# Two chunks split around a third, and attention output strips in turn, in a fused attention and MLP kernel

## The chip, the cores and the metric

The kernel runs on one core of a Trainium2 chip. Its engines are TensorE (PE, matrix products into PSUM), VectorE (DVE), ScalarE (ACT), GpSimd (POOL) and SyncE (SP, here the queue that issues every transfer). The metric is device time in microseconds (us) of one execution, as the median of several runs.

## The reference

A gated linear attention (4 batches, 8 heads, 768 time steps, head dimension 48) is followed by two MLPs over 3072 tokens of 384 features with 2048 hidden features: the first has the activation h * tanh(softplus(h)), the second relu(h) squared.

```python
for t in range(S):
    state = alpha[:, :, t, :, None] * state + np.einsum('bhd,bhe->bhde', k[:, :, t], v[:, :, t])
    y[:, :, t] = np.einsum('bhd,bhde->bhe', q[:, :, t], state)
...
h = x @ w_in
g = h * np.tanh(np.log1p(np.exp(h)))
x = g @ w_out
...
h = np.maximum(x @ w_in2, 0.0)
out = h * h @ w_out2
```

## The kernel before

**Staging.** Time is cut into 6 chunks (`c`) of 128 steps; a chunk holds 4 blocks, one per batch (`b`), so 512 tokens. The attention of one block is a handful of functions: `a_load` and `a_loadv` fetch alpha, k, q (one tile `akq`) and v; `a_prep`, `a_inv` and `a_k` run the cumulative products on DVE (two scans, three multiplications); `a_kT` transposes k on PE; `a_scores` forms the scores on PE and masks them on DVE (tiles `at`, two for a block); `a_y` forms the output on PE; `a_u` updates the running state `st`; `a_x` splits the output into a high and a low part (`xh`, `xl`), which the first MLP reads. Every f32 product of the MLPs is made from three matmuls of such parts.

**The MLP steps.** A step is one chunk `c` and one inner tile `f` of 128 hidden features (16 for each MLP). `h_mm` makes 9 matmuls into a PSUM bank `ph` (three banks), `mish1` to `mish3` or `relu1` run on ACT and DVE, `split_hi` and `split_lo` write `gh` and `gl`, and `out1` adds 9 matmuls into the accumulators `pc` of the chunk (`out2`, of the second MLP, 12 narrower ones). The first MLP has 96 steps in the order `STEPS1`, the second 96 in the order `STEPS`. The weights come as 64-bit floats in pairs of inner tiles and are turned into two f32 parts (`w_load`, `w_sign`, `w_abs`, `w_bits`, `w_split`, the last writing `whi` on ACT and `wlo` on DVE).

**What splits a chunk.** Before, chunk 0 runs its first 8 inner tiles, then chunk 1 all 16, then chunk 0 the other 8; its half sum waits in DRAM (`x2d`) and is fetched by `p_load`:

```python
STEPS1 = STEPS[:HALF] + STEPS[NF:2 * NF] + STEPS[HALF:NF] + STEPS[2 * NF:]
```

The tiles `xh` and `xl` have two buffers each, so that two chunks of attention output are held at a time.

**The order.** Nothing is issued as it is written. A `Plan` records every call, and its `order` gives each engine a fixed list: among the calls whose inputs it reckons ready, it picks by earliest start within `SLACK` and then by a key, from tables of numbers (`FIRST_AT`, `EARLY_AT`, `LATER_AT`, `WEIGHT_AT`, `MLP_AT`). The engines then run their lists in order, and SP its transfers.

**The attention output.** `a_y` fills a bank of 3 column blocks (`kk`) by 4 strips (`i`) of 32 output rows. In the first two blocks a strip takes a matmul from the state (not in chunk 0) and one from the masked scores of its head; in the third one from the state and two from scores. The strips are written one after the other:

```python
for i in range(4):
    ...
    if c > 0:
        nc.tensor.matmul(o, s2, qt[c, b][:, p, :], start=True, stop=False, skip_group_check=True)
    for h in heads:
        nc.tensor.matmul(o, w, at[c, b, j][:, p, :], ...)
```

Of the kernel before, what the change touches and what calls it, by code (L numbers as in the profile page):

```python
# [9 lines left out]
F32 = mybir.dt.float32  # L10
F32R = mybir.dt.float32r
# [16 lines left out]
LAG = 3  # L28
# [7 lines left out]
FIRST, EACH = -14.34, 4.47
FIRST_AT = dict(a_load=-8.92, a_loadv=-0.87, a_prep=-25.04, a_inv=-1.22, a_k=-40.25, a_kT=16.99, a_scores=-42.12, a_flag=-25.48, a_y=-7.03, a_u=-55.34, a_x=19.72)
EARLY_AT = dict(a_load=86.48, a_loadv=0.29, a_prep=-2.05, a_inv=1.20, a_k=-0.59, a_kT=-39.22, a_scores=-50.37, a_flag=29.17, a_y=-26.49, a_u=-16.63, a_x=-15.63)
LATER_AT = dict(a_load=-106.20, a_loadv=-63.70, a_prep=-101.21, a_inv=20.99, a_k=37.87, a_kT=-78.32, a_scores=-75.84, a_flag=23.67, a_y=2.78, a_u=-20.53, a_x=-24.76, b_load=-9.08, p_load=53.41)
WEIGHT_AT = dict(w_load=-16.99, w_sign=-7.37, w_abs=-52.56, w_bits=-0.61, w_split=-4.57)  # L40
MLP_AT = dict(mish1=42.39, mish2=0.64, mish3=1.90, hi=1.97, lo=-28.42, out=0.86)
EXP20 = 485165195.40979
NG = NF // 2

HALF = NF // 2
STEPS = [(c, f) for c in range(NBLK) for f in range(NF)]
STEPS1 = STEPS[:HALF] + STEPS[NF:2 * NF] + STEPS[HALF:NF] + STEPS[2 * NF:]
SEG = CH + 1
NALPHA = NP * SEG + 1
NROW = NALPHA + 2 * NP * CH  # L50
# [151 lines left out]
class Plan:  # L202
# [42 lines left out]
    def order(self):  # L245
        units = self.units
        users = {name: {i for i, _, _ in self.uses[name]} for name in self.tag_of}
        left = {name: len(x) for name, x in users.items()}
        nth, made, begun, freed = {}, {}, {}, {}
        for u in units:  # L250
            for name in u["new"]:
                tag = self.tag_of[name][0]
                nth[name] = made.get(tag, 0)
                made[tag] = nth[name] + 1
        held = [[] for _ in units]
        for name, x in users.items():
# [12 lines left out]

        def buffers(i):  # L270

            t, seen = 0.0, {}
            for name in units[i]["new"]:
                tag, bufs = self.tag_of[name]
                n = begun.get(tag, 0) + seen.get(tag, 0)
                seen[tag] = seen.get(tag, 0) + 1
                if nth[name] != n or len(freed.get(tag, [])) <= n - bufs:
                    return None
                if n >= bufs:
                    t = max(t, sorted(freed[tag])[n - bufs])  # L280
            return t

        for _ in units:
            picks = []
            for q, pool in ready.items():
                found = []
                for i in pool:
                    t = buffers(i)
                    if t is not None:
                        found.append((max(free[q], base[i], t, shared if units[i]["port"] else 0.0), units[i]["key"], i))  # L290
                if found:
                    first = min(found)[0]
                    pick = min((x for x in found if x[0] <= first + SLACK[q]), key=lambda x: x[1:])
                    picks.append((first, q, pick))
            _, q, (t, _, i) = min(picks, key=lambda x: x[0])
            u = units[i]
            ready[q].discard(i)
            start[i] = t
            free[q] = t + u["cost"] + (SWITCH if u["mode"] != mode and q == "P" else 0.0)
            mode = u["mode"] or mode  # L300
            done[i] = free[q] + u["late"]
            if u["port"]:
                shared = free[q] + (0.08 if q == "V" else 0.0)
            for name in u["new"]:
                tag = self.tag_of[name][0]
                begun[tag] = begun.get(tag, 0) + 1
            for name in held[i]:
                left[name] -= 1
                if not left[name]:
                    freed.setdefault(self.tag_of[name][0], []).append(max(done[j] for j in users[name]))  # L310
            for j in after[i]:
                base[j] = max(base[j], done[i] if i in units[j]["deps"] else start[i])
                wait[j] -= 1
                if not wait[j]:
                    ready[units[j]["queue"]].add(j)
        return sorted(range(len(units)), key=lambda i: start[i])
# [30 lines left out]
def price(queue, op, args, kw):  # L347
# [6 lines left out]
    if queue == "P":  # L354
        if op == "transpose":
            return 0.109, 0.2, False
        m, n = args[1].free_size(), args[2].free_size()
        if args[2].dtype == F32R:
            return n / 2200, 0.2, False
        return (0.085 if m == 32 else 0.052 if n == D else 0.107), 0.28, False  # L360
# [34 lines left out]
def fast_kernel(ctx, tc, flags, akq, v, w1i, w1o, w2i, w2o, out):  # L395
# [142 lines left out]
    def a_y(c, b):  # L538
        ps = abank(c, 2)
        for kk in range(NK):  # L540
            for i in range(4):
                o = ps[32 * i:32 * i + 32, CH * kk:CH * kk + CH]
                heads = (4 * kk + i,) if kk < 2 else (2 * i, 2 * i + 1)
                if c > 0:
                    p = heads[0] // 2
                    s2 = st[:, b, p, heads[0] % 2, CUT[heads[0] % 2][0]] if kk < 2 else st[:, b, p].rearrange("p j e -> p (j e)")[:, 32:64]
                    nc.tensor.matmul(o, s2, qt[c, b][:, p, :], start=True, stop=False, skip_group_check=True)
                for h in heads:
                    p, j = h // 2, h % 2
                    w = vt[c, b][:, h, CUT[j][1] if kk < 2 else CUT[j][2]]  # L550
                    nc.tensor.matmul(o, w, at[c, b, j][:, p, :], start=(c == 0 and h == heads[0]), stop=(h == heads[-1]), skip_group_check=True)
        yt[c, b] = ps

    def a_u(c, b):
# [25 lines left out]


    hps, ut, dy, gt, gh, gl = {}, {}, {}, {}, {}, {}
    acc, stage, part = {}, {}, None

    def mm3(ps, wpair, xhi, xlo, first, last):
        whi, wlo = wpair
# [42 lines left out]
        gl[c, f] = lo  # L629

    def out1(c, f):
        half = c == 0 and f >= HALF
        first, last = f in (0, HALF * half), f in (NF - 1, HALF - 1 if c == 0 else NF - 1)
        if first:
            acc[c] = [bank(psc, "pc") for _ in range(NK)]
        whi, wlo = wt[1, f]
# [2 lines left out]
            s = slice(128 * kk, 128 * kk + 128)  # L639
            mm3(acc[c][kk], (whi[:, s], wlo[:, s]), hi, lo, first, last)  # L640
        if last:
            t = part if half else stp.tile([128, NK, BT], F32, tag="stage", name="x2")
# [7 lines left out]
            nc.sync.dma_start(x2d[c], t)  # L650

    def p_load(c):
        nonlocal part
        part = stp.tile([128, NK, BT], F32, tag="stage", name="x2")
        nc.sync.dma_start(part, x2d[c])

    def b_load(c):
        hi = xp.tile([128, NK, BT], F32R, tag="xh", name="xh")
# [47 lines left out]
    with tc.manual_schedule():  # L706
# [13 lines left out]
        def at_step(t, fn, *args, key=None):  # L720
            name = fn.__name__
            if key is None:
                c, b = args[0], args[1] if len(args) > 1 else 0
                if c == 0 and name[0] == "a":
                    key = FIRST + EACH * b + FIRST_AT[name]
                else:
                    key = t + (EARLY_AT if 0 < c < 3 and name[0] == "a" else LATER_AT)[name]
            slots.setdefault(math.floor(t), []).append((fn, args, key))

        def wanted(m, g):  # L730
            return (STEPS if m > 1 else STEPS1).index((int(m < 2 and g >= NG // 2), 2 * g)) + LAG * (m % 2) + NA * (m // 2)

        def w_tasks(t, m, g):
            need = wanted(m, g)
# [15 lines left out]
            at_step(t + 5, a_x, 0, b)  # L750
        for c in range(1, NBLK):
            for b in range(B):
                t = (2 * b - 6, 2 * b + 17)[c - 1] if c < 3 else 16 * (c - 1) + 4 * b - 5
                at_step(max(t - 2, -7), a_load, c, b)
                at_step(max(t - 2, -7), a_loadv, c, b)
                at_step(t, a_prep, c, b)
# [111 lines left out]
```

## Time and profile before

| what | value |
|---|---|
| median of 3 runs | 965.78 us (963.88 to 966.77) |
| the profiled execution | 966.28 us, of which its span is 964.6 us |
| PE busy | 934.1 us |
| DVE busy | 637.3 us |
| ACT busy | 559.6 us |
| mean granted TensorE clock | 0.982 |

The span runs from the first to the last instruction of the profiled execution; 1.7 us of its own time lie outside it. PE is busy nearly throughout on the average, so that the time is to be read by stretches: where PE stands, and what it waits for there.

### The profile page before, as it was taken

What the parts mean: (1) busy time and instruction counts of PE and PEld (TensorE: products, weight loads), DVE (VectorE), ACT (ScalarE), POOL (GpSimd) and SP (SyncE); (2) the same over time, 40 slices, a digit from 0 to 9 for tenths busy, and PEclk for the clock granted to TensorE, in tenths of its full rate; (3) what the DMA queues carried; (4) which work ended last, traced back from release to release, by engine and by line L of the source; (5) the groups of instructions that cost most, each with busy time, mean ns of one, the idle gap of its engine ahead of it and who ended that gap; (6) DMA issues with size and microseconds to landing.
All of it is one profiled execution on the core that took longest, in us unless ns stands there. A gap on an engine that the chain in (4) does not pass through costs nothing.

```text
span 964.6 us, 14441 instructions
## 1 busy us (share of the span) xinstructions
PE 934.1 (97%) x5818; PEld 788.5 (82%) x5818; DVE 637.3 (66%) x1014; ACT 559.6 (58%) x1103; POOL 2.7 (0%) x10
## 2 busy tenths in 40 slices
PE   6888999999999999999999999999999999999996
PEld 5666777778888888878888889988999899999995
DVE  7899999998788887777679997343333343433332
ACT  4487998778666767677599865332332332422322
POOL 1000000000000000000000000000000000000000
PEclk7699999999999999999999999999999999999998
DMA  8145324340221211121032251010000100100001
GB/s 326 68 154 191 126 66 137 121 149 1 82 82 47 77 45 45 44 78 45 1 138 92 70 194 64 1 66 1 33 33 1 66 1 1 66 1 1 34 1 36
DMA packets 22075, 67.13 MB, mean 70 GB/s; under 512 B 1776, under 2 KB 4848, under 8 KB 22000
## 3 DMA queue, kind: packets, MB, share of 16 engines
q1 hardware_dynamic: 22000, 66.13, 19.6%
q8 instruction: 47, 0.77, 0.3%
q14 instruction: 28, 0.23, 0.1%
HBM read 55.90 MB, written 10.22 MB: 69 GB/s over the span
## 4 chain that ended last, share of the span: by engine, by line
PE 83%; ACT 7%; DVE 7%; issue 1%; DMA 1%; SPq 0%; DVEq 0%; ACTq 0%
PE ph L321 37%; PE pc L321 34%; PE pa L321 12%; ACT u L321 2%; ACT y L321 2%; ACT raw L321 1%; DVE akq L321 1%; ACT whi L321 1%; DVE raw L321 1%; DMA raw<-w1o 1%; DVE P L321 1%; DVE st L321 1%; ACT gh L321 1%; DVE gl L321 1%; ACT akq L321 1%
## 5 line engine op out<-in xcount | busy, mean ns | idle before, releaser
L321 PE MATMUL ph<-xh,wlo 128*128 128x512 f32 x576 | 230.1, 399 | 5.3 <-DVE g L321 2.7
L321 PE MATMUL ph<-xh,whi 128*128 128x512 f32 x576 | 228.0, 396 | 0.0
L321 PE MATMUL ph<-xl,whi 128*128 128x512 f32 x576 | 227.9, 396 | 0.0
L321 DVE TENSOR_TENSOR gl<-g,gh 128x512 fp32r<-128x512 f32 x192 | 131.9, 687 | 127.2 <-ACT gh L321 126.7
L321 ACT ACTIVATE u<-ph 128x512 f32<-128x512 f32 x192 | 113.8, 593 | 170.0 <-PE ph L321 163.4
L321 ACT ACTIVATE gh<-g 128x512 fp32r<-128x512 f32 x192 | 120.2, 627 | 135.1 <-PE pa L321 112.8
L321 DVE TENSOR_TENSOR g<-u,ph 128x512 f32<-128x512 f32 x96 | 66.0, 687 | 118.6 <-ACT u L321 118.6
L321 PEld LDWEIGHTS ph<-xh,wlo 128*128 128x128 f32 x576 | 108.7, 189 | 28.7 <-DVE g L321 4.4
L321 PEld LDWEIGHTS ph<-xh,whi 128*128 128x128 f32 x576 | 108.5, 188 | 25.4
L321 PEld LDWEIGHTS ph<-xl,whi 128*128 128x128 f32 x576 | 108.5, 188 | 20.6
L321 PE MATMUL pc<-gh,wlo 128*128 128x512 f32 x288 | 117.0, 406 | 0.9 <-ACT x L321 0.9
L321 PE MATMUL pc<-gh,whi 128*128 128x512 f32 x288 | 113.6, 394 | 0.0
L321 PE MATMUL pc<-gl,whi 128*128 128x512 f32 x288 | 113.1, 393 | 0.0
L321 DVE SCALAR_TENSOR_TENSOR u<-u,y 128x512 f32<-128x512 f32 x96 | 65.8, 686 | 50.4 <-ACT y L321 50.1
L321 PE MATMUL pc<-wlo,gh 128*128 128x384 f32 x288 | 97.0, 337 | 0.0
L321 PE MATMUL pc<-whi,gh 128*128 128x384 f32 x288 | 97.0, 337 | 0.0
L321 PE MATMUL pc<-whi,gl 128*128 128x384 f32 x288 | 96.9, 337 | 0.0
L321 DVE SCALAR_TENSOR_TENSOR g<-y,ph 128x512 f32<-128x512 f32 x96 | 65.4, 681 | 1.6
L321 PEld LDWEIGHTS pc<-gh,wlo 128*128 128x128 f32 x288 | 54.1, 188 | 14.8 <-ACT x L321 1.3
L321 DVE SCALAR_TENSOR_TENSOR y<-u,y 128x512 f32<-128x512 f32 x96 | 65.7, 685 | 0.7
L321 PEld LDWEIGHTS pc<-gh,whi 128*128 128x128 f32 x288 | 54.0, 187 | 13.2
L321 PEld LDWEIGHTS pc<-gl,whi 128*128 128x128 f32 x288 | 54.1, 188 | 12.1 <-DVE gl L321 0.6
(90 smaller groups left out, 1261.6 us busy)
## 6 DMA issues: line engine op xcount, KB each, us to landing
akq<-akq SPq DMA_DIRECT2D x20, 770.5 KB, 4.5
raw<-w1i SPq DMA_DIRECT2D x8, 768.0 KB, 4.6
v<-v SPq DMA_DIRECT2D x24, 256.0 KB, 4.4
raw<-w1o SPq DMA_DIRECT2D x8, 768.0 KB, 4.3
raw<-w2i SPq DMA_DIRECT2D x8, 768.0 KB, 4.4
raw<-w2o SPq DMA_DIRECT2D x8, 768.0 KB, 4.3
x2d<-x SPq DMA_DIRECT2D x7, 768.0 KB, 3.5
x<-x2d SPq DMA_DIRECT2D x7, 768.0 KB, 4.3
```

The lines of the kernel that those rows point to most:

```text
L321: method(*args, **kw)
```

## The change

Chunks 0 and 1 each run their first 8 inner tiles (steps 0 to 15), then chunk 2 all 16 (steps 16 to 31), then chunk 1 and chunk 0 their other 8 (steps 32 to 47); from chunk 3 on, the order stays. Since two buffers cannot hold three chunks, `x_keep` writes chunk 0's `xh` and `xl` to DRAM and `x_load` fetches them again, and chunk 1 now has a half sum to store and fetch as well. Chunk 2's attention is due 15 steps earlier than it was, the second half of the first MLP's weights 8 steps later. In `a_y` the four strips of a column block take turns: all state matmuls, then all first score matmuls, then all second ones. The planner's tables are new throughout, its price of a 32-row matmul is 0.06 in place of 0.085, and it counts two calls on PE, one behind the other, as free of the latency between them. The numbers of the tables decide the order and are not shown beyond a line.

```diff
-SLACK = dict(P=4.68, V=0.01, A=0.18, G=0.10, S=3.45)
+SLACK = dict(P=0.00, V=0.00, A=0.04, G=0.10, S=0.60)
...
-MLP_AT = dict(mish1=42.39, mish2=0.64, mish3=1.90, hi=1.97, lo=-28.42, out=0.86)
+MLP_AT = dict(mish1=-42.55, mish2=5.46, mish3=2.38, hi=8.43, lo=-0.03, out=3.78)
...
-HALF = NF // 2
+HALF, SPLIT = NF // 2, 2
 STEPS = [(c, f) for c in range(NBLK) for f in range(NF)]
-STEPS1 = STEPS[:HALF] + STEPS[NF:2 * NF] + STEPS[HALF:NF] + STEPS[2 * NF:]
+STEPS1 = [(c, f) for c in (0, 1) for f in range(HALF)] + [(2, f) for f in range(NF)]
+STEPS1 += [(c, f) for c in (1, 0) for f in range(HALF, NF)] + STEPS[3 * NF:]
...
+            groups = [(4 * kk + i,) if kk < 2 else (2 * i, 2 * i + 1) for i in range(4)]
+            o = [ps[32 * i:32 * i + 32, CH * kk:CH * kk + CH] for i in range(4)]
+            for i, heads in enumerate(groups if c > 0 else ()):
...
+                nc.tensor.matmul(o[i], s2, qt[c, b][:, p, :], start=True, stop=False, skip_group_check=True)
+            for n in range(len(groups[0])):
+                for i, heads in enumerate(groups):
...
-        half = c == 0 and f >= HALF
+        split = c < SPLIT
+        half = split and f >= HALF
...
+    def x_keep(c):
+        for x, d in zip((xh[c], xl[c]), x0d):
+            nc.sync.dma_start(d, x.bitcast(F32))
+
+    def x_load(c):
+        xh[c], xl[c] = (xp.tile([128, NK, BT], F32R, tag=name, name=name) for name in ("xh", "xl"))
+        for x, d in zip((xh[c], xl[c]), x0d):
+            nc.sync.dma_start(x.bitcast(F32), d)
...
-                t = (2 * b - 6, 2 * b + 17)[c - 1] if c < 3 else 16 * (c - 1) + 4 * b - 5
+                t = (2 * b - 6, 2 * b + 2, 2 * b + 33)[c - 1] if c < 4 else 16 * (c - 1) + 4 * b - 5
...
-        at_step(2 * NF - 2, p_load, 0)
+        at_step(HALF, x_keep, 0)
+        at_step(2 * NF, x_load, 0)
+        at_step(2 * NF + 4, p_load, 1)
+        at_step(2 * NF + HALF + 4, p_load, 0)
```

**On PE, in the third column block of `a_y`.** Before, for chunk 1's first block (`pa` is the output bank, `akq,st` the state matmul, `at,v` a score matmul), the first two of four strips:

```order
L321 MATMUL pa_209<-akq_159,st_109 32x128
L321 MATMUL pa_209<-at_197,v_160 32x128
L321 MATMUL pa_209<-at_198,v_160 32x128
L321 MATMUL pa_209<-akq_159,st_109 32x128
L321 MATMUL pa_209<-at_197,v_160 32x128
L321 MATMUL pa_209<-at_198,v_160 32x128
```

The same block in the change, with the last matmul of the second column block ahead of it and the state update behind it:

```order
L323 MATMUL pa_211<-at_200,v_162 32x128
L323 MATMUL pa_211<-akq_161,st_109 32x128 x4
L323 MATMUL pa_211<-at_199,v_162 32x128 x4
L323 MATMUL pa_211<-at_200,v_162 32x128 x4
L323 MATMUL pa_212<-v_162,kT_196 64x48 x8
```

Three matmuls of one strip stood together; now four of a kind, each of another strip, stand together.

**On DVE, ahead of the masked scores of a late attention block.** Before, the rows up to the second mask of chunk 2's last block (`at_488`, `at_489`), which stand behind 28 `h_mm` and 24 `out1` on PE; there are 293 rows up to here:

```order
L321 SCALAR_TENSOR_TENSOR y_454<-u_452,y_454 128x512
L321 TENSOR_SCALAR raw_995<-raw_995 128x768
L321 SCALAR_TENSOR_TENSOR g_469<-y_454,ph_451 128x512
L321 SCALAR_TENSOR_TENSOR raw_995<-raw_995 128x768
L321 SCALAR_TENSOR_TENSOR P_490<-akq_464,reset_108 128x516
L321 TENSOR_SCALAR x2_472<-pc_323 128x512
L321 TENSOR_TENSOR akq_464<-akq_464,P_490 128x512
L321 TENSOR_TENSOR at_488<-pa_486,mask_107 128x512
L321 TENSOR_TENSOR at_489<-pa_487,mask_107 128x512
```

In the change, the rows up to the second mask of chunk 3's first block (`at_571`, `at_572`), behind 33 `h_mm` and 27 `out1` on PE; there are 330 rows up to here:

```order
L323 TENSOR_TENSOR gl_504<-g_501,gh_503 128x512
L323 RECIPROCAL reset_108<-P_551 128x4
L323 SCALAR_TENSOR_TENSOR u_506<-u_506,y_508 128x512
L323 TENSOR_TENSOR gl_510<-g_507,gh_509 128x512
L323 SCALAR_TENSOR_TENSOR y_508<-u_506,y_508 128x512
L323 TENSOR_TENSOR akq_533<-akq_533,P_551 128x512
L323 TENSOR_TENSOR at_571<-pa_569,mask_107 128x512
L323 TENSOR_TENSOR at_572<-pa_570,mask_107 128x512
```

All of chunk 2's attention, which before stood between steps 18 and 28, now stands ahead of step 16, and chunk 3's last three blocks stand between steps 42 and 48.

**On SP, around the fetch of chunk 0's kept input.** In the change, with `x2_541` chunk 2's result and `x2_560` the half sum of chunk 1:

```order
L323 DMA raw_1018<-w2o 128x2x768
L323 DMA xh_524<-x0d0_110 128x1536
L323 DMA xl_525<-x0d1_111 128x1536
L323 DMA akq_552<-akq 128x1541
L323 DMA x2d2_114<-x2_541 128x1536
L323 DMA x2_560<-x2d1_113 128x1536
L323 DMA v_553<-v 128x512
```

The fetch waits for the last `h_mm` that reads chunk 2's `xh` (step 31), whose buffer it takes; the store of chunk 2's result, the fetch of chunk 1's half sum and chunk 3's later loads are queued behind it.

## Rows read from the trace of the kernel before

**Rows 1.** The page: span, then busy time, share and instructions of each engine.
```profile
span 964.6 us, 14441 instructions
...
PE 934.1 (97%) x5818; PEld 788.5 (82%) x5818; DVE 637.3 (66%) x1014; ACT 559.6 (58%) x1103; POOL 2.7 (0%) x10
```

**Rows 2.** Busy time by stretches: length, each engine (instructions), granted clock, DMA share.
```profile
0.00:42.49 42.49, 30.77 (x316) 24.53 (x317) 34.86 (x59) 19.31 (x40) 2.66 (x10) 0.73 0.57 206
42.49:133.71 91.22, 83.06 (x610) 64.72 (x609) 87.26 (x140) 76.53 (x152) 0.00 (x0) 0.98 0.43 150
133.71:201.13 67.42, 65.62 (x503) 51.53 (x503) 64.99 (x107) 56.56 (x117) 0.00 (x0) 1.00 0.32 109
201.13:225.14 24.01, 24.00 (x174) 19.24 (x174) 23.86 (x42) 17.19 (x37) 0.00 (x0) 1.00 0.29 102
225.14:547.40 322.26, 322.26 (x2174) 260.16 (x2173) 255.12 (x418) 235.99 (x475) 0.00 (x0) 1.00 0.17 61
```

**Rows 3.** PE's timeline at chunk 2's last block: start, duration, instruction, idle time and releaser.
```profile
201.13 0.42 PE L321 MATMUL pa<-akq,st 128*32 128x128 f32 x4 [0.77 <-DVE at L321]
```

**Rows 4.** PE's timeline through one attention output and the state update behind it.
```profile
239.85 0.45 PE L321 MATMUL pa<-akq,st 128*32 128x128 f32 x8
...
240.31 0.44 PE L321 MATMUL pa<-akq,st 128*32 128x128 f32 x8
...
240.75 0.38 PE L321 MATMUL pa<-akq,st 128*32 128x128 f32 x2
...
242.25 0.67 PE L321 MATMUL pa<-v,kT 128*64 128x48 f32 x16
242.85 0.50 PE L321 MATMUL pc<-gh,wlo 128*128 128x512 f32 x1
243.19 0.39 PE L321 MATMUL pc<-gl,whi 128*128 128x512 f32 x1
```

**Rows 5.** PE's timeline at a transposition of k and at the scores.
```profile
206.63 0.63 PE L321 MATMUL pa<-ident,akq 128*128 128x128 f32 x4
207.01 0.48 PE L321 MATMUL ph<-xh,wlo 128*128 128x512 f32 x1
...
209.30 1.16 PE L321 MATMUL pa<-akq 48*128 48x128 f32 x16
210.39 0.50 PE L321 MATMUL pc<-gh,wlo 128*128 128x512 f32 x1
```

**Rows 6.** PE's timeline at its last matmul of the second MLP.
```profile
955.30 0.34 PE L321 MATMUL pa<-whi,gh 128*128 128x384 f32 x1
```

**Rows 7.** The chain that ended last: one step's `h_mm`, one `out1`: start, us, what.
```profile
223.21 2.09 PE pc L321 x9
225.30 2.09 PE ph L321 x9
```

**Rows 8.** DVE's timeline where it runs without a break.
```profile
65.88 0.95 DVE L321 SCALAR_TENSOR_TENSOR raw<-raw 128x768 int32<-128x768 int32 x1
66.75 0.68 DVE L321 SCALAR_TENSOR_TENSOR y<-u,y 128x512 f32<-128x512 f32 x1
67.35 0.68 DVE L321 SCALAR_TENSOR_TENSOR u<-u,y 128x512 f32<-128x512 f32 x1
...
69.15 1.22 DVE L321 TENSOR_TENSOR_SCAN P<-akq,reset 128x516 f32<-128x516 f32 x1
70.29 0.66 DVE L321 SCALAR_TENSOR_TENSOR g<-y,ph 128x512 f32<-128x512 f32 x1
...
72.40 0.34 DVE L321 TENSOR_TENSOR st<-st,pa 64x192 f32<-64x192 f32 x1
72.67 0.68 DVE L321 TENSOR_TENSOR gl<-g,gh 128x512 fp32r<-128x512 f32 x1
```

**Rows 9.** DMA issues by kind: count, KB each, us from issue to landing.
```profile
x2d<-x SPq DMA_DIRECT2D x7, 768.0 KB, 3.5
x<-x2d SPq DMA_DIRECT2D x7, 768.0 KB, 4.3
```

More of the change, by code (lines that the diff above doesn't have):

```diff
@@ L32 @@
 BYTE_SHIFTS = range(8)
-SLACK = dict(P=4.68, V=0.01, A=0.18, G=0.10, S=3.45)
[L36 to L40, printed above, removed]
-MLP_AT = dict(mish1=42.39, mish2=0.64, mish3=1.90, hi=1.97, lo=-28.42, out=0.86)
+SLACK = dict(P=0.00, V=0.00, A=0.04, G=0.10, S=0.60)
+FIRST, EACH = -18.51, 1.95
+FIRST_AT = dict(a_load=-10.28, a_loadv=-6.32, a_prep=-5.60, a_inv=-5.08, a_k=-12.87, a_kT=22.41, a_scores=4.85, a_flag=79.31, a_y=-5.96, a_u=40.39, a_x=27.07)
+EARLY_AT = dict(a_load=-15.47, a_loadv=-42.21, a_prep=3.06, a_inv=3.92, a_k=-33.68, a_kT=-51.78, a_scores=-5.31, a_flag=-34.88, a_y=-38.93, a_u=3.94, a_x=-2.21)
+LATER_AT = dict(a_load=11.61, a_loadv=-15.13, a_prep=-5.26, a_inv=16.58, a_k=0.90, a_kT=-32.26, a_scores=-34.40, a_flag=-8.77, a_y=-1.60, a_u=-26.88, a_x=78.23, b_load=6.26, p_load=-50.04, x_keep=-25.45, x_load=-0.15)
+WEIGHT_AT = dict(w_load=-25.97, w_sign=-3.64, w_abs=53.00, w_bits=0.06, w_split=-0.32)
+MLP_AT = dict(mish1=-42.55, mish2=5.46, mish3=2.38, hi=8.43, lo=-0.03, out=3.78)
 EXP20 = 485165195.40979
 NG = NF // 2
-HALF = NF // 2
+HALF, SPLIT = NF // 2, 2
 STEPS = [(c, f) for c in range(NBLK) for f in range(NF)]
-STEPS1 = STEPS[:HALF] + STEPS[NF:2 * NF] + STEPS[HALF:NF] + STEPS[2 * NF:]
+STEPS1 = [(c, f) for c in (0, 1) for f in range(HALF)] + [(2, f) for f in range(NF)]
+STEPS1 += [(c, f) for c in (1, 0) for f in range(HALF, NF)] + STEPS[3 * NF:]
 SEG = CH + 1
@@ L311, in order @@
             for j in after[i]:
-                base[j] = max(base[j], done[i] if i in units[j]["deps"] else start[i])
+                same = units[j]["queue"] == "P" == u["queue"]
+                base[j] = max(base[j], free["P"] if same else done[i] if i in units[j]["deps"] else start[i])
                 wait[j] -= 1
@@ L359, in price @@
             return n / 2200, 0.2, False
-        return (0.085 if m == 32 else 0.052 if n == D else 0.107), 0.28, False
+        return (0.06 if m == 32 else 0.052 if n == D else 0.107), 0.28, False
     if queue == "S":
@@ L418, in fast_kernel @@
     st = const.tile([128, B, NP, 2, D], F32, name="st")
+    x0d = [dram.tile([128, NK, BT], F32, name=f"x0d{i}") for i in range(2)]
     x2d = [dram.tile([128, NK, BT], F32, name=f"x2d{i}") for i in range(NBLK)]
@@ L540, in a_y @@
         for kk in range(NK):
[L541 to L548, printed above, removed]
+            groups = [(4 * kk + i,) if kk < 2 else (2 * i, 2 * i + 1) for i in range(4)]
+            o = [ps[32 * i:32 * i + 32, CH * kk:CH * kk + CH] for i in range(4)]
+            for i, heads in enumerate(groups if c > 0 else ()):
+                p, j = heads[0] // 2, heads[0] % 2
+                s2 = st[:, b, p, j, CUT[j][0]] if kk < 2 else st[:, b, p].rearrange("p j e -> p (j e)")[:, 32:64]
+                nc.tensor.matmul(o[i], s2, qt[c, b][:, p, :], start=True, stop=False, skip_group_check=True)
+            for n in range(len(groups[0])):
+                for i, heads in enumerate(groups):
+                    h = heads[n]
                     p, j = h // 2, h % 2
                     w = vt[c, b][:, h, CUT[j][1] if kk < 2 else CUT[j][2]]
-                    nc.tensor.matmul(o, w, at[c, b, j][:, p, :], start=(c == 0 and h == heads[0]), stop=(h == heads[-1]), skip_group_check=True)
+                    nc.tensor.matmul(o[i], w, at[c, b, j][:, p, :], start=(c == 0 and n == 0), stop=(h == heads[-1]), skip_group_check=True)
         yt[c, b] = ps
@@ L582, in fast_kernel @@
     hps, ut, dy, gt, gh, gl = {}, {}, {}, {}, {}, {}
-    acc, stage, part = {}, {}, None
+    acc, stage, parts = {}, {}, {}
     def mm3(ps, wpair, xhi, xlo, first, last):
@@ L631, in out1 @@
     def out1(c, f):
-        half = c == 0 and f >= HALF
-        first, last = f in (0, HALF * half), f in (NF - 1, HALF - 1 if c == 0 else NF - 1)
+        split = c < SPLIT
+        half = split and f >= HALF
+        first, last = f == HALF * half, f in (NF - 1, HALF - 1 if split else NF - 1)
         if first:
@@ L641, in out1 @@
         if last:
-            t = part if half else stp.tile([128, NK, BT], F32, tag="stage", name="x2")
+            t = parts.pop(c) if half else stp.tile([128, NK, BT], F32, tag="stage", name="x2")
             for kk in range(NK):
@@ L652, in p_load @@
     def p_load(c):
-        nonlocal part
-        part = stp.tile([128, NK, BT], F32, tag="stage", name="x2")
-        nc.sync.dma_start(part, x2d[c])
+        parts[c] = stp.tile([128, NK, BT], F32, tag="stage", name="x2")
+        nc.sync.dma_start(parts[c], x2d[c])
+    def x_keep(c):
[5 more added lines that the diff above has]
+            nc.sync.dma_start(x.bitcast(F32), d)
     def b_load(c):
@@ L726, in at_step @@
                 else:
-                    key = t + (EARLY_AT if 0 < c < 3 and name[0] == "a" else LATER_AT)[name]
+                    key = t + (EARLY_AT if 0 < c < 4 and name[0] == "a" else LATER_AT)[name]
             slots.setdefault(math.floor(t), []).append((fn, args, key))
         def wanted(m, g):
-            return (STEPS if m > 1 else STEPS1).index((int(m < 2 and g >= NG // 2), 2 * g)) + LAG * (m % 2) + NA * (m // 2)
+            return (STEPS.index((0, 2 * g)) if m > 1 else min(n for n, (_, f) in enumerate(STEPS1) if f == 2 * g)) + LAG * (m % 2) + NA * (m // 2)
         def w_tasks(t, m, g):
```

## The prediction

> **What bounds the kernel now.** I read the page first: PE is busy for 97% of the span [rows 1]. Such an average hides where PE stands, so the stretches come next. The reader is to see that two kinds of time follow each other. Up to 201.13 us DVE is the engine without room: it is busy for 87.26 of 91.22 us and then for 64.99 of 67.42, while PE is busy for 83.06 and 65.62 [rows 2]. From 201.13 on PE is busy in 24.00 of 24.01 us and then in all of 322.26, with DVE at 255.12 [rows 2], and its last MLP matmul starts at 955.30 [rows 6]. The border is an event: at 201.13 chunk 2's last `a_y` begins after 0.77 us of waiting for the masked scores `at` of DVE [rows 3]. It is the last time that PE waits for DVE to any amount. So
>
> time = (when DVE lets PE past its last wait) + (PE work behind that) + tail.
>
> The last matmul starts at 955.30 and the next would start 0.17 later, so PE is done with the MLPs at 955.5; 9.1 us of span and 1.7 us outside it follow, and the change touches neither.
>
> **PE's prices.** One step's `h_mm` and one `out1` take 2.09 each [rows 7]; I use 2.09 for `out2` too. A transposition of k costs 207.01 - 206.63 = 0.38, the scores of a block 210.39 - 209.30 = 1.09 [rows 5], the state update 242.85 - 242.25 = 0.60, an `a_y` 242.25 - 239.85 = 2.40 [rows 4]. Where PE changes from narrow tiles to full ones, the next full matmul follows 0.34 later (243.19 - 242.85 [rows 4]) in place of 2.09/9 = 0.23, so each of these pieces costs 0.1 more.
>
> Check on before. At 201.13 the order has let 28 `h_mm` and 24 `out1` past; 164 and 168 are left, 332 x 2.09 = 693.9. Left of the attention: 13 `a_y` (31.2), 9 state updates (5.4), 12 transpositions (4.6), 12 scores (13.1), 46 edges (4.6), together 58.9. Sum 752.8; the trace has 955.5 - 201.1 = 754.4. So 1.6 us are lost in 750.
>
> **Term 1: strips in turn.** The 2.40 us of `a_y` are not spread evenly. The first two column blocks, 16 matmuls, take 240.75 - 239.85 = 0.90; the third, 12 matmuls, takes 242.25 - 240.75 = 1.50 [rows 4]. In the first two, eight records of state matmuls stand in one piece although the order alternates state and score: strips overtook one another there, with one matmul of a strip waiting behind another. With two waiting (the third block) they did not; the stretch of rows x1 and x2 there is a staggered queue. In turn, no strip ever has two matmuls in a row. I price the third block by the first two: 12 x 0.90/16 = 0.675. `a_y` becomes 1.575 and 0.825 us are saved, 20 times (chunk 0's `a_y` has no state matmul and keeps the pattern that already runs well): 16.5 us of PE work. Bounds: nothing, if the 1.50 has another reason, and no more than 16.5: a strip does its two matmuls of a block in 0.45, so its three take 0.675 even where all four strips run at once.
>
> The Trainium skill's page "TensorE: Matmul & The Clock Gate", section "Measured speedup vs the span model", gives three column tiles 2.38x, not 3x. If four strips overlapped only at that 79%, the third block would take 0.675/0.79 = 0.85 by an estimate from this page, and the saving would be 13 us. The rows of the first two blocks show no such loss, so I keep 16.5 and hold the other as a rival.
>
> **Term 2: when DVE lets PE past.** The change reorders DVE's work, so I count what stands ahead. Spacings of DVE instructions, start to start [rows 8]: 512 elements 0.60 (67.35 - 66.75), 768 elements 0.87 (66.75 - 65.88), a scan 1.14 (70.29 - 69.15), a state update 0.27 (72.67 - 72.40); 384 elements I estimate at 0.45 by their length.
>
> Before, up to the mask that PE waits for: 154 of 512 (92.4), 50 of 768 (43.5), 25 scans (28.5), 36 state updates (9.7), 11 of 384 (5.0), small ones 2.9; sum 182.0. DVE's busy time to 201.13 is 34.86 + 87.26 + 64.99 = 187.1 [rows 2], 2.8% more, and it idles for 7.6 us before 42.49 and 6.4 in the 158.6 us behind [rows 2].
>
> After, the comparable place is chunk 3's first `a_y`, behind 33 `h_mm` and 27 `out1`: DVE has 177 of 512 (106.2), 48 of 768 (41.8), 27 scans (30.8), 40 updates (10.8), 12 of 384 (5.4), small 2.2 ahead, sum 197.2. With the same 2.8%: 202.7; idle 7.6 at the start and 0.040 a us until then, 7.0. It is through at 217.3. Chunk 2's attention, now ahead of step 16, is four blocks more of DVE work there, but the second half of the weights moves behind it in exchange, and by step 32 the two sums have met again.
>
> PE work behind it: 159 + 165 = 324 x 2.09 = 677.2; 12 `a_y` at 1.575 (18.9), 8 state updates (4.8), 11 transpositions (4.2), 11 scores (12.0), 42 edges (4.2). Sum 721.3, with the 1.6 lost as before 722.9.
>
> **Term 3: chunk 3 squeezed.** From step 41 to 52 the order gives DVE 39.3 us of attention and 44 x 0.60 = 26.4 of activation, 65.7; PE has 66.7 us. Equal loads wait for each other now and then; I allow 1.0 us. Without DVE's lead there it would be 65.7 x 1.068 = 70.2 against 66.7 (2.8% and 0.040 as above), so at most 3.5.
>
> **Terms at nothing.** `x_keep`, `x_load` and the second half sum are six transfers of 768 KB at 3.5 or 4.3 us [rows 9]. They run beside transfers that take 0.43 to 0.29 of the engines' time [rows 2]. SP is in order, so what is queued behind matters. `x_keep` waits for chunk 0's last `xl`, which stands on DVE ahead of the masks of chunk 1's first block, while the next `akq` load behind it needs that block's buffer anyway. `x_load` can start after step 31, and step 40 needs it 36 us of PE work later; two transfers take 8.6. Without that cover PE would stand those 8.6 us at step 40. The half sums have as long.
>
> **Sum.** 217.3 + 722.9 + 1.0 = 941.2 against 955.5: 14.3 less, 952.0 for the profiled execution of 966.28. The median of the runs shown is 0.5 below that execution, so I predict **951.5**. A difference under 0.3% (2.9 us) is about what a measurement of this kernel can't tell from no change.
>
> **Rivals.**
> - *DVE waits less than before* in its new order: half the idle behind 42.49 gives 951.5 - 3.5 = 948. For: DVE's list has more attention to fill gaps with. Against: ACT, too, is busy 76.53 of 91.22 [rows 2], and DVE's gaps are waits for it.
> - *DVE bounds PE again* in steps 41 to 52: 951.5 + 2.5 = 954, with late loads behind the store of chunk 2's result up to 957. Chunk 3's last blocks come one right after the other, with scores masked only some 2 us ahead of `a_y`.
> - *The strips overlap in part*: 951.5 + 3.5 = 955.
> - *The strips gain nothing* and the change does not do what it says on PE: 951.5 + 16.5 = 968. Against it stand the 16 matmuls in 0.90 us.
> - *Slower*: chunk 2's attention and chunk 1's are both wanted in the first 16 steps, where DVE, ACT and PE hang on each other block by block. Each us that DVE idles more ahead of 217.3 is one us of the end. It decides at 14.3 more, 28.9 us of idle in place of 14.6; at 20 more the time is 971. For it speaks only that stretch's crowding; before, idle grew by 6.4 in 158.6 us.
>
> **How the numbers follow.** Chances: the forecast (948.5 to 954) 0.55; DVE again, or the strips in part (954 to 959), 0.20; DVE waits less (945 to 948.5) 0.12; idle growing by 8 to 14 us (959 to 965.8) 0.06; slower through DVE 0.04, strips without gain 0.03. The likeliest is 951.5. The range 946 to 959 leaves out 0.13 above and some 0.04 below; the likeliest case alone spans 948.5 to 954. Below 962.9 (faster by over 0.3%) lie 0.91, within 0.3% (to 968.7, strips without gain among them) 0.05, above 0.04.
>
> **What would show it.** An `a_y` of chunk 1 on should take 1.5 to 1.7 us on PE, its third block about 0.7. PE's last wait for `at` or `gl` of more than 0.5 us should lie at 212 to 222 us, and PE should be busy without a break behind it. `x_load` should land before 235. I am wrong in term 1 if `a_y` stays above 1.9; in term 2 if PE stands behind 225; in term 3 if it stands near steps 41 to 52 (about 250 to 330) for over 3 us.

## The result, and the profile after

The changed kernel takes 957.84 us (median of 4 runs, 955.87 to 958.36) against 965.25 of the kernel before (4 runs beside it): ratio 0.9919 [0.9897, 0.9941], 7.4 us faster. I had predicted 951.5, 14.3 less: the direction was right and half of the gain is missing; the time lies inside the range of 946 to 959, in the branch from 954 to 959 that had a chance of 0.20. The profiled execution took 958.34 us.

The page after, with the lines that answer to [rows 1]:

```profile
span 956.4 us, 14433 instructions
...
PE 927.8 (97%) x5818; PEld 780.4 (82%) x5818; DVE 636.3 (67%) x1017; ACT 554.2 (58%) x1103; POOL 2.7 (0%) x10
```

The stretches of [rows 2], now of the changed kernel (length, busy time of PE, its weight loads, DVE, ACT and POOL, granted clock, DMA share, GB/s):

```profile
0.00:42.49 42.49, 33.02 (x348) 26.98 (x352) 35.10 (x61) 18.36 (x40) 2.66 (x10) 0.64 0.66 242
42.49:133.71 91.22, 83.53 (x744) 64.81 (x736) 86.24 (x144) 70.80 (x146) 0.00 (x0) 0.91 0.42 148
133.71:201.13 67.42, 67.19 (x422) 53.32 (x421) 65.27 (x103) 59.28 (x121) 0.00 (x0) 1.00 0.34 114
201.13:225.14 24.01, 24.01 (x165) 19.16 (x165) 23.96 (x40) 21.39 (x46) 0.00 (x0) 1.00 0.47 165
225.14:547.40 322.26, 319.58 (x2142) 254.24 (x2141) 265.09 (x436) 237.72 (x482) 0.00 (x0) 1.00 0.21 72
```

Two things are new. In 42.49 to 133.71 the granted clock is 0.91 where it was 0.98. And behind 225.14, where PE was busy without a break before, it now stands for 322.26 - 319.58 = 2.7 us.

PE's timeline through one undisturbed `a_y`, to be read beside [rows 4] (a record group's start, duration, instruction), with the full matmul ahead of it:

```profile
323.08 0.40 PE L323 MATMUL pc<-gh,whi 128*128 128x512 f32 x1
323.41 0.43 PE L323 MATMUL pa<-akq,st 128*32 128x128 f32 x8
323.65 0.40 PE L323 MATMUL pa<-at,v 128*32 128x128 f32 x8
323.87 0.40 PE L323 MATMUL pa<-akq,st 128*32 128x128 f32 x8
324.09 0.40 PE L323 MATMUL pa<-at,v 128*32 128x128 f32 x8
324.31 0.40 PE L323 MATMUL pa<-akq,st 128*32 128x128 f32 x8
324.53 0.62 PE L323 MATMUL pa<-at,v 128*32 128x128 f32 x16
325.08 0.67 PE L323 MATMUL pa<-v,kT 128*64 128x48 f32 x16
```

It takes 325.08 - 323.41 = 1.67 us in place of 2.40. The third column block, 1.50 before, takes 325.08 - 324.31 = 0.77. Every group of four strips starts 0.22 to 0.24 behind the one ahead of it (two records a matmul), in the third block as in the first two. One full-width matmul of 128 columns takes as long in e8 below (24 in 5.28 us, 0.22 each), so the four strips overlap fully. The last row of the block takes 0.55: two groups at 0.22, and 0.11 on the way to the next piece.

PE's and DVE's timelines where chunk 3's first `a_y` begins (the place that answers to [rows 3]), and PE's last matmul ([rows 6]):

```profile
218.81 0.43 PE L323 MATMUL pa<-akq,st 128*32 128x128 f32 x8
...
947.35 0.34 PE L323 MATMUL pa<-whi,gh 128*128 128x384 f32 x1
```
```profile
216.90 1.28 DVE L323 TENSOR_TENSOR at<-pa,mask 128x512 f32<-128x512 f32 x2
```

The masks end at 216.90 + 1.28 = 218.18, PE comes at 218.81 and does not wait: there is no bracket with idle time at that row, where [rows 3] has 0.77.

**PE's lost time.** To see where time goes I take the start of a step's `h_mm` and subtract PE's work ahead of it at its durations in the traces (2.09 for `h_mm` and `out1`, 1.09, 0.38 and 0.60 for scores, transposition and state update, 1.67 or 2.40 for `a_y`, 1.23 for chunk 0's, 6.9 for the warm-up, 0.1 for each narrow piece). What is left is time that PE lost up to there, dummy matmuls of an experiment included. One profiled execution of each kernel (steps count from 0):

| kernel | step 8 | 16 | 42 | 58 | 180 | median us | ratio to before |
|---|---|---|---|---|---|---|---|
| before | 29.0 | 31.9 | 35.4 | 35.6 | 36.4 | 965.25 | |
| changed | 34.2 | 36.4 | 36.9 | 42.4 | 43.3 | 957.84 | 0.9919 |
| e1 | 31.5 | 34.5 | 40.7 | 41.5 | 42.9 | 958.75 | 0.9932 |
| e2 | 30.0 | 30.3 | 30.5 | 32.5 | 33.5 | 963.27 | 0.9986 |
| e3 | 31.8 | 34.6 | 35.5 | 38.2 | 39.2 | 954.05 | 0.9889 |
| e4 | 33.4 | 36.2 | 36.8 | 42.3 | 43.9 | 957.00 | 0.9909 |
| e5 | 29.4 | 32.5 | 33.0 | 36.0 | 36.9 | 954.04 | 0.9882 |
| e6 | 30.6 | 33.7 | 36.2 | 38.2 | 39.3 | 956.36 | 0.9906 |
| e7 | 31.2 | 34.3 | 35.2 | 37.6 | 38.6 | 955.37 | 0.9895 |
| e8 | 31.3 | 34.2 | 34.7 | 41.3 | 43.1 | 958.10 | 0.9925 |
| e9 | 31.9 | 34.8 | 35.7 | 39.4 | 40.4 | 956.94 | 0.9916 |
| e10 | 32.6 | 34.8 | 35.3 | 40.8 | 41.7 | 957.45 | 0.9918 |
| e11 | 30.6 | 33.7 | 34.2 | 39.7 | 40.7 | 954.93 | 0.9890 |
| e12 | 29.9 | 33.0 | 33.9 | 36.5 | 38.0 | 953.82 | 0.9878 |

The first two rows account for the result: twenty `a_y` save 20 x 0.73 = 14.6 us of PE work, and PE loses 43.3 - 36.4 = 6.9 us more, so 7.7 less; the profiled executions differ by 966.28 - 958.34 = 7.9. In the changed kernel PE loses nearly nothing between steps 16 and 42, and then 5.5 us between 42 and 58, where before lost 0.2.

The places in that stretch, by PE's timeline (idle time ahead of a row and what ended it in brackets):

```profile
287.95 0.63 PE L323 MATMUL pa<-ident,akq 128*128 128x128 f32 x4 [0.90 <-PE pa L323]
298.94 0.51 PE L323 MATMUL ph<-xl,whi 128*128 128x512 f32 x1 [0.40 <-DVE xl L323]
317.39 0.63 PE L323 MATMUL pa<-ident,akq 128*128 128x128 f32 x4 [0.56 <-PE pc L323]
347.63 0.63 PE L323 MATMUL pa<-ident,akq 128*128 128x128 f32 x4 [0.81 <-issue]
```

These four are 2.7 of the 5.5 us. Another 1.0 lies inside `a_y`, which there take up to 2.04 in place of 1.67 without a bracket. Of the remaining 1.8, some 0.8 is no waiting at all: the table prices a narrow piece at 0.1, but where it stands between full matmuls it costs about 0.1 at either end (323.08 to 323.41 above is 0.33, in place of 0.23). Between steps 42 and 58 the changed kernel's 27 narrow pieces stand in 20 separate groups; at the border prices of its undisturbed stretches that makes 3.5 us where the table counts 2.7. Before has 16 pieces in 12 groups there and spends 1.9 where the table counts 1.6. The last 1.0 is spread over full matmuls that start late, again without a bracket.

DVE's timeline ahead of the first of these places, and the scalings of k ahead of the third and the fourth:

```profile
283.77 0.68 DVE L323 SCALAR_TENSOR_TENSOR x<-pc,x 128x512 f32<-128x512 f32 x1
284.37 0.68 DVE L323 TENSOR_TENSOR gl<-g,gh 128x512 fp32r<-128x512 f32 x1
284.97 0.68 DVE L323 SCALAR_TENSOR_TENSOR x<-pc,x 128x512 f32<-128x512 f32 x1
285.57 1.22 DVE L323 TENSOR_TENSOR_SCAN akq<-akq,reset 128x516 f32<-128x516 f32 x1
286.71 0.53 DVE L323 TENSOR_TENSOR xl<-pa,xh 128x384 fp32r<-128x384 f32 x1
287.16 0.69 DVE L323 TENSOR_TENSOR akq<-akq 128x512 f32<-128x512 f32 x1
...
316.60 0.69 DVE L323 TENSOR_TENSOR akq<-akq 128x512 f32<-128x512 f32 x1
...
346.85 0.68 DVE L323 TENSOR_TENSOR akq<-akq 128x512 f32<-128x512 f32 x1
```

The transposition at 287.95 reads the k that DVE scales at 287.16 and finishes at 287.85; the profile names another instruction of PE, which had long been done. The other two transpositions, too, begin 0.10 behind the scaling of their k. DVE runs without a break ahead of each of the three, and ahead of the first two additions of chunk 1's half sum (`x<-pc,x`) stand in its queue.

### The profile page after: what moved, and what is told of

Same layout as the page of the kernel before. It is cut to its first block, busy times and chain, and to the rows that moved or that the text cites. A ratio compares the mean times of both kernels' runs of the same rounds, so it can differ in the third digit from the quotient of the medians.

```text
span 956.4 us, 14433 instructions
## 1 busy us (share of the span) xinstructions
PE 927.8 (97%) x5818; PEld 780.4 (82%) x5818; DVE 636.3 (67%) x1017; ACT 554.2 (58%) x1103; POOL 2.7 (0%) x10
## 4 chain that ended last, share of the span: by engine, by line
PE 82%; DVE 12%; ACT 2%; issue 1%; DMA 1%; SPq 0%
PE ph L323 39%; PE pc L323 34%; PE pa L323 10%; DVE akq L323 3%; DVE P L323 1%; DVE st L323 1%; DVE at L323 1%; DVE gl L323 1%; DVE y L323 1%; DVE g L323 1%; DVE u L323 1%; DVE raw L323 1%; DMA v<-v 1%; DMA raw<-w1i 1%; ACT u L323 1%
## 5 line engine op out<-in xcount | busy, mean ns | idle before, releaser
L323 PEld LDWEIGHTS ph<-xh,wlo 128*128 128x128 f32 x576 | 108.9, 189 | 29.9 <-DVE g L323 3.7
L323 DVE SCALAR_TENSOR_TENSOR u<-u,y 128x512 f32<-128x512 f32 x96 | 65.8, 686 | 34.4 <-ACT y L323 33.7
```

Source lines behind the costliest of these rows:

```text
L323: method(*args, **kw)
```

## Experiments: the two halves of the change apart

Only `a_y` is exchanged between the two kernels, by the lines of the diff above; every other instruction keeps its place in its own kernel's order.

**e1**, before with the new strips:

```diff
-            for i in range(4):
 ...
-                for h in heads:
 ...
+            for n in range(len(groups[0])):
+                for i, heads in enumerate(groups):
 ...
```

> The kernel before with its own order, tables and half sums, in which only the matmuls of a_y go to the four strips in turn; no other instruction moves. Theory A (strips give 0.73 us for each a_y, PE is the bound only behind 201 us there): the 13 a_y behind 201.13 us save 13 x 0.73 = 9.5 us, the 7 ahead of it hide behind DVE: 965.25 - 9.5 = 955.8, between 950.7 (all 20 count) and 957; that is as fast as the changed kernel or faster, so its new order gives nothing. Rival B (the new order is needed for the gain): 960 or more. Rival C (strips gain nothing): 965.

Measured 958.75 (0.9932 [0.9912, 0.9951]): 6.2 less than 964.99, the median of before in that comparison; the profiled executions differ by 966.28 - 958.01 = 8.3. The median lies between A's range (up to 957) and B's (960 or more). By the lost time A has the mechanism: up to step 42 it grows from 35.4 to 40.7, so the seven `a_y` there (7 x 0.73 = 5.1) gave nothing. A is too rich, as 1.2 us more are lost behind (2.2 in place of 1.0). C falls, and so does B: e1 is within 1 us of the changed kernel, with intervals that overlap, so most of the gain doesn't need the new order.

**e2**, the changed kernel with the old strips (the same edit backwards):

> The changed kernel with a_y's matmuls in their old order, strip by strip; no other instruction moves. Theory A: the 12 a_y behind 218.8 us cost 0.73 us more each, 8.8 us, less what hides in the 5.3 us that PE waits in steps 43 to 57 (up to four a_y, 2.9 us); those ahead of 152 us hide behind DVE: 957.84 + 5.9 to 8.8 = 963.7 to 966.6, so the new order alone is worth about nothing against 965.25. Rival B (the order carries the gain): under 961. Rival C: 957.8.

Measured 963.27 (0.9986 [0.9972, 0.9999]). The new order alone is worth 0.14%, and its interval only just excludes no gain; the strips on top of it are worth 963.27 - 957.84 = 5.4, just below what A gave: twelve `a_y` cost 8.8 us of PE work more, and 3.4 of it disappears in PE's waits, which between step 42 and the end are 3.0 in place of 6.4. The parts add: 0.9932 x 0.9986 = 0.9918.

The new order does something else than it seems. By step 42 it loses 5 us less than the old one (30.5 against 35.4, both with the old strips); behind step 42 it loses 3.0, the old one 1.0.

## Experiments: where steps 42 to 58 lose their time

**e3**, chunk 3's state updates early:

```diff
-                    at_step(t + 6, a_u, c, b)
+                    at_step(t + 6, a_u, c, b, key=t + 1 if c == 3 else None)
```

> The changed kernel in which chunk 3's four state updates have the key t + 1 in place of t + 9.94, so that the first one runs in step 34 in place of 43, and chunk 3's later blocks and chunk 4's first two come some 2 to 4 steps earlier, into the stretch in which DVE idles (steps 35 to 43, about 10 us). Theory A (the missing 6 us are PE's waits for a DVE that has too much to do in steps 43 to 57 because the attention comes late): 2 to 5 us less, 953 to 956. Rival D (the same work is just as crowded earlier): 957 to 959. Rival E (the missing time lies in the added transfers or in a_y): no change, 957.8.

Measured 954.05 (0.9889 [0.9869, 0.9909]): in A's range, and D and E fall. The loss between steps 42 and 58 is 2.7 in place of 5.5; this profile was also 1.8 us ahead at step 16, where both kernels are the same, so that not all of the 3.8 us comes from the key. The buffer `kT` is single (`ktp` has one), so what the next block's transposition gives can't be stored until this update has read it; with its key of 42.9 it held chunk 3's second block until step 43.

**e4**, the added transfers twice:

```diff
             nc.sync.dma_start(d, x.bitcast(F32))
+            nc.sync.dma_start(d, x.bitcast(F32))
 ...
             nc.sync.dma_start(x.bitcast(F32), d)
+            nc.sync.dma_start(x.bitcast(F32), d)
```

> The changed kernel in which each transfer of x_keep and of x_load is made twice (four more transfers of 768 KB on the same queue, 3.5 to 4.3 us each); PE's order is the same. Theory A (these transfers are hidden): 957.8, within 1.5. Rival E (they are what costs the missing 6 us, as loads queued behind them come late): 961 or more.

Measured 957.00 (0.9909 [0.9892, 0.9926]), inside A's range: the transfers are hidden, E falls again.

**e5**, five short scans:

```diff
+        if (3, 0) < (c, b) < (4, 2):
+            nc.units[-1]["calls"][0] = (..., (back[:, :8], back[:, :8], ...), ...)
```

The scan is priced in full by the planner, so that the order stays, and issued over 8 elements.

> The changed kernel in which five backward scans of DVE (chunk 3's blocks 1 to 3, chunk 4's blocks 0 and 1) run over 8 elements in place of 516: some 5 x 1.0 us less work for DVE between 264 and 335 us, every instruction in its place. It leaves out most of the inverse decay of these five blocks. Theory A1 (in steps 43 to 57 PE waits because DVE has too much work there): the PE time lost in these steps falls from 5.5 us to between 1.5 and 3, so 954 to 956. Theory A2 (PE waits there for hand-overs from one engine to the next and for its two narrow PSUM banks, not for DVE's amount of work): within 1 us of 957.8.

Measured 954.04 (0.9882 [0.9861, 0.9903]); 3.0 us are lost between steps 42 and 58. Part of the 957.84 - 954.04 comes from elsewhere: this profile was already 3.9 us ahead at step 16, where both kernels are the same (below). But the 2.5 us less of loss in that stretch are DVE's. One of the five scans runs at 215.4 in this profile, ahead of the stretch; four lie in it. The windows show what they do (changed kernel, then e5, in the columns above): PE stands 1.86 of 85 us, then 0.10.

```profile
225.14:255.00 29.86, 29.86 (x131) 24.13 (x130) 23.93 (x38) 25.92 (x53) 0.00 (x0) 1.00 0.14 54
255.00:340.00 85.00, 83.14 (x802) 64.26 (x802) 74.84 (x135) 53.69 (x113) 0.00 (x0) 1.00 0.25 85
```
```profile
255.00:340.00 85.00, 84.90 (x817) 66.24 (x816) 74.60 (x143) 54.22 (x115) 0.00 (x0) 1.00 0.32 106
```

At 287.95 and 317.39 in the changed kernel PE waits for a block whose scan is short in e5, and there it no longer waits. The transposition at 347.63 is that of chunk 4's last block, whose scan e5 leaves whole, and its wait stays (behind the window, in e5):

```profile
341.23 0.63 PE L323 MATMUL pa<-ident,akq 128*128 128x128 f32 x4 [0.83 <-issue]
```

A short scan takes work off DVE and also brings k of its own block sooner, so e5 by itself doesn't tell the amount of work from the length of the chain; that DVE runs without a break ahead of these waits speaks for the amount.

In e3 DVE works earlier: it does 3.5 us more ahead of 255, where it idled for 5.9 us in the changed kernel.

```profile
225.14:255.00 29.86, 29.86 (x154) 23.64 (x153) 27.46 (x46) 25.24 (x55) 0.00 (x0) 1.00 0.18 63
```

**e6**, the x buffer one chunk earlier (on top of e3):

```diff
-        at_step(2 * NF, x_load, 0)
 ...
+        n = 1 if m == 0 and c == 0 and f >= HALF else m * NBLK + c
 ...
```

`n` is the chunk whose x `h_mm` reads.

> The kernel with chunk 3's early state updates, in which also chunk 0's x is not loaded back: its second half reads chunk 1's x in its place (so these partial sums are left out and others added), and chunk 3's x gets the buffer that chunk 2 leaves at step 31 in place of chunk 1's at step 39. PE's order now spreads chunk 3's attention over steps 33 to 43. If the two x buffers are what crowds chunk 3's attention behind step 40, the 2.7 us that PE still lost in steps 42 to 56 fall to 1 or less: 951.5 to 953. If DVE's amount of work alone is the limit there, no change: 954.

Measured 956.36 (0.9906 [0.9888, 0.9925]), above both expectations: no gain over e3. PE's order spread as meant, but the loss only moved ahead: 1.6 us of it now lie between steps 38 and 40. The two x buffers are not the cause by themselves.

**e7**, three weight groups of the second MLP late (on top of e3):

```diff
+        if m > 1 and g < 3:
+            nc.units[-1]["deps"].add(nc.steps[60])
 ...
```

> The kernel with chunk 3's early state updates, in which the loads of the second MLP's first three weight groups wait for step 60, so that their nine DVE instructions (6.6 us between 221 and 246, needed only in step 96) leave the stretch in which DVE is full. Theory A1 (DVE's amount of work): up to 2.5 us less, 951.5 to 953. Theory A2 (these instructions fill time in which nothing else of DVE's is ready, since chunk 3's x waits for its buffer): within 0.7 us of 954.

Measured 955.37 (0.9895 [0.9878, 0.9912]): no gain. It is 1.4 above 954 and so outside A2's 0.7 too; by the ratios to before it is 0.6 us above e3. Between 218 and 260 us DVE is busy for 33.5 of 42 us where e3 has 39.5: these instructions filled time that nothing else of DVE's used. They stand ahead of step 42, so e7 says nothing on the amount of work behind it.

What settles: in steps 42 to 58 PE waits for a DVE queue with too much attention work in it, of which one key makes a good part late. Some 2.7 to 3 us remain by the table in e3 and e5. Of these, 0.7 to 0.8 in each is the price of the borders. Of the rest, e3 has 1.5 us of waits that the trace shows, and two of its three longest are of the same kind as above: transpositions at 283.84 and 299.20, each 0.10 behind the scaling of its k, with DVE busy without a break for over 10 us ahead. DVE itself had stood for 2.57 us ahead of 262.60, until a load of `akq` landed; whether that load could come earlier is open, as no run moves it.

## Experiments: the clock behind a wait of 2.9 us

In the changed kernel PE waits for a weight group at step 6, and what happens behind it differs between executions of the same instructions. PE's timeline of the changed kernel, and of e5 (the same instructions up to there), from that wait to the next `a_y`:

```profile
84.33 0.80 PE L323 MATMUL ph<-xh,wlo 128*128 128x512 f32 x1 [2.93 <-DVE wlo L323]
...
95.19 0.43 PE L323 MATMUL pa<-akq,st 128*32 128x128 f32 x8
```
```profile
83.45 0.51 PE L323 MATMUL ph<-xh,wlo 128*128 128x512 f32 x1 [2.82 <-DVE wlo L323]
...
90.36 0.43 PE L323 MATMUL pa<-akq,st 128*32 128x128 f32 x8
```

The same pieces take 10.86 us in the one and 6.91 in the other. The windows from 83 to 94 us give the granted clock (changed kernel; e5; e10, the changed kernel again; e11):

```profile
83.00:94.00 11.00, 9.66 (x34) 7.56 (x35) 8.34 (x14) 6.54 (x13) 0.00 (x0) 0.53 0.44 143
```
```profile
83.00:94.00 11.00, 10.22 (x116) 8.16 (x117) 10.91 (x19) 9.64 (x20) 0.00 (x0) 1.00 0.46 147
```
```profile
83.00:94.00 11.00, 10.05 (x54) 7.71 (x58) 9.51 (x18) 6.86 (x14) 0.00 (x0) 0.69 0.44 143
```
```profile
83.00:94.00 11.00, 10.22 (x122) 8.17 (x121) 10.91 (x19) 8.44 (x18) 0.00 (x0) 1.00 0.45 144
```

At 0.53 PE runs nearly all of it at the lower of its two levels, and DVE, which sets the pace here, falls from 10.91 to 8.34 of 11 us because its input is late:

```profile
91.78 0.69 DVE L323 TENSOR_TENSOR at<-pa,mask 128x512 f32<-128x512 f32 x1 [2.63 <-PE pa L323]
```

**e8, e9, e11, e12**: dummy matmuls fill the wait, 24 in e8 and e9, 11 in e11 and e12; e9 and e12 on top of e3. **e10** is the changed kernel once more.

```diff
         whi, wlo = wt[m, f]
+        if (m, c, f) == (0, 0, 6):
+            nc.tensor.matmul(ps[:, :128], ident, ident, start=True, stop=True)
+            nc.units[-1]["calls"] *= 24
 ...
```

Expected of e8, e9 and e10, in this order:

> The changed kernel with 24 dummy matmuls (identity by identity, 128 columns) ahead of step 6's h_mm, written into the bank that it then overwrites; nothing else moves. They fill the 2.9 us that PE waits there for a weight group (81.4 to 84.3 us). Theory F (after that wait the granted clock falls to 0.50 until 93 us in some executions, as in the profiled one, and the pieces there take 4 us longer; DVE runs dry and all behind it comes later): the clock stays at 1.00 between 83 and 94 us, step 8 begins near 95 to 97 us in place of 99.6, and the median is 1 to 3 us lower, 955 to 957; the slowest executions gain most. Rival: the fall has no price, since DVE is the bound there: 957.8 as the same kernel run beside it.

> Chunk 3's state updates early and the 24 dummy matmuls ahead of step 6 together, to see whether the two gains add: 954.05 - 1 to 2.5 = 951.5 to 953 if they do (in the profile of the kernel with the early updates the clock fell to 0.66 between 85 and 90 us); 954 if not.

> The changed kernel once more, unaltered, beside the two others on the same chip: 957.8, within 1.5. In executions with a lower mean clock the time should be longer: about 958.3 at 0.972 to 0.975 and 956 at 0.982, as in the first four.

e10 came out at 957.45 (0.9918 [0.9905, 0.9932]) and agrees with the first runs; its slowest execution, 959.37, has the lowest clock, 0.971, but the order of the others does not follow the clock. e8 at 958.10 (0.9925 [0.9911, 0.9939]) and e9 at 956.94 (0.9916 [0.9903, 0.993]) missed: the clock stayed at 1.00 between 83 and 94 us in both, but 24 dummies took 5.28 us, 0.22 each, and `h_mm` came some 2 us late; what e8 had gained by step 16 was lost again behind step 42 (8.4 us there, 6.4 in e10). I had sized them by a rate that was half of that.

Expected of e11 and then of e12:

> The changed kernel with 11 dummy matmuls ahead of step 6's h_mm in place of 24. The 24 took 5.28 us (0.22 each) and so delayed that h_mm by some 2 us; 11 take 2.4 us and fit into the wait of 2.9. Theory F (the fall of the granted clock behind that wait costs time): clock 1.00 between 83 and 94 us, step 8 at 95 to 96 us, PE's lost time at step 8 some 2 to 4 us less than in the changed kernel, and a median of 955.5 to 957. If the DVE-full stretch of steps 43 to 57 swallows it: 957 to 958 with step 8 early all the same.

> Chunk 3's state updates early and the 11 dummy matmuls together. Without the 24's delay: 952.5 to 954 if the clock's fall cost these executions time as well; 954 to 955.5 if not. As the fastest correct version so far 954.05 (0.989 of the kernel before) is to be beaten or repeated.

e11 takes 954.93 (0.9890 [0.9873, 0.9906], 954.45 to 956.12): 2.5 less than e10 (2.7 by the ratios, each to runs of before beside it) and 0.6 below its forecast, with the clock at 1.00; all its runs are faster than all of e10's. Its lost time, dummies included, is 30.6 at step 8 against 32.6 in e10 and 34.2 in the changed kernel's first profile. F holds here: the fall costs 2.0 and 3.6 us at step 8 in these two profiles, of which 1.0 and 2.6 are left at step 180. e12 takes 953.82 (0.9878 [0.9861, 0.9894]), the lowest median of all, and faster than both kernels. Over e3 alone, in whose profile the clock fell too, it gains no more than the measurement can tell, so that the price of the fall is shown by e11 alone.

## Why the prediction was right in direction and wrong in size

PE is done with the MLPs at 947.35 + 0.17 = 947.5 in place of 941.2: 6.3 us more, which the three terms take up.

- **Term 1, strips in turn.** Right in mechanism, mis-sized by 0.095: `a_y` takes 1.67, not 1.575. I scaled the whole 1.50 of the third block by the first two, but its end holds 0.11 on the way to the next piece, which the first two don't have. Twelve `a_y` behind the border: 12 x 0.095 = 1.1 us. The rival of partly overlapping strips falls: the groups start every 0.22 throughout. The Trainium skill's 2.38x for three column tiles (page "TensorE: Matmul & The Clock Gate", section "Measured speedup vs the span model") does not show here: 0.85 by that estimate against 0.77 measured, of which 0.11 is the exit. The page's figure is for 512 columns, these matmuls have 128.
- **Term 2, when DVE lets PE past.** 218.81 for 217.3, 1.5 late. The step's picture was wrong all the same. PE does not wait at that place; its last wait ahead of step 42 ends in step 15 (0.22 us, at 146.98), and from step 16 on PE and DVE are both full and arrive together, the masks at 218.18. So the "last wait of more than 0.5 us at 212 to 222" was not there. What made PE late is mostly the clock's fall behind step 6, which the sum did not have: in e10, with a shorter fall, and in e11, without one, step 32 begins at 214.9 and 213.85 in place of 216.5. In the profiles without a fall (e5, e6, e7, e11) chunk 3's first `a_y` begins at 214.9 to 216.7, which is 0.6 to 2.4 ahead of the forecast. So that DVE's account came out to the digit in its idle time (203.6 us of work for 202.7, and 14.6 of idle for 14.6, up to 218.18) is luck in part: the idle time holds the fall.
- **Term 3, chunk 3 squeezed.** This is the step that was sized wrong. I allowed 1.0, at most 3.5; behind 218.81 PE needs 947.5 - 218.8 = 728.7 us where 722.9 + 1.0 were forecast, 4.8 more, 1.1 of them from term 1. The 3.7 left belong here; counted the other way, PE loses 6.4 us behind step 42 where 1.6 + 1.0 were allowed. Between steps 42 and 58 alone it is 5.5, and 4.3 by step 52, where over 3 was the sign of being wrong (1.9 of it as idle time in the trace). I compared the loads of steps 41 to 52 as a sum, 65.7 against 66.7. But DVE's queue is in order and its work comes in blocks, so PE waits at single pieces although the sums fit, and the stretch goes on to step 57. e3 and e5 show that these waits are DVE's. About 0.8 us of the 5.5 is no wait: the sum prices a narrow piece at 0.1 however it stands, and the squeezed order sets more pieces apart (20 groups in place of 12). The rival "DVE bounds PE again", 954 with up to 957, is what happened; its "late loads" are not (e4).
- **Terms at nothing.** The transfers were priced rightly (e4): the row below puts `x_load`'s second transfer at 5.9 us; issued at 215.9, it landed at 221.8, ahead of the 235 that I asked for. That the second half sums also put three additions of 0.60 each into DVE's fullest stretch was not in those terms.

```profile
xh<-x0d SPq DMA_DIRECT2D x1, 768.0 KB, 4.2
xl<-x0d SPq DMA_DIRECT2D x1, 768.0 KB, 5.9
```

By parts: my sum holds 12 x 0.825 = 9.9 us for the strips and so 4.4 for the order; measured, the order alone gives 1.7 (e2) and the strips on top of it 5.4. 1.1 + 1.5 + 3.7 = 6.3 closes the account, as the 3.7 is what the other two leave.

## What to carry to other kernels

A saving on an engine counts only where that engine is the bound: eight of the changed kernel's twenty shorter attention outputs vanished in waits, and more than a third of what the other twelve saved was lost again in the stretch where the other engine was full. When work of two engines is compared over a stretch, sums that fit are not enough if both queues are in order; look at the single pieces that are handed over, and at the key that sets the first of them. A column of lost time by step finds such a place in one pass, and one moved key gave back half of what the stretch lost. Such a column holds every error of its prices, too: compare it with the idle time that the trace shows before calling all of it waiting.

## What the runs showed of the hardware

The same wait of PE was followed by a lower granted clock in some executions and not in others: of the eight profiles without dummy matmuls in it, five fell (the changed kernel after 2.93 us, e2 after 2.25, e3 after 2.84, e4 and e10 after 3.11) and three did not (e5 after 2.82, e6 after 2.94, e7 after 2.91). Where it fell for longest, the pieces behind took 10.86 us in place of 6.91. The Trainium skill (page "TensorE: Matmul & The Clock Gate", section "HAM oscillation — how this bites in real kernels") tells of a kernel in which the wait between two bursts of matmuls puts PE back to half rate every time; the five falls agree with it in kind, the three profiles that kept the clock show that a wait need not do so. With dummy matmuls in the wait the clock was 1.00 between 83 and 94 us in all four profiles, 11 of them in e11 and e12, 24 in e8 and e9.

Four matmuls on four strips of 32 output rows, issued in turn, took 0.22 us together, as long as one full-width matmul of the same 128 columns (0.22 in e8). In the old order, with two matmuls of a strip waiting one behind the other, the 12 matmuls of the third column block took 1.50 us in place of 0.77.
